# Ten tiles' transposes of p: from TensorE to 32x32 blocks on VectorE and a pass through DRAM

## The chip, the cores and the metric

The kernel runs on one core of a Trainium2 chip, as one program. The metric is the device time of an execution in microseconds (us). Times of a kernel are given as the median of a few executions, with the lowest and highest. One execution each is recorded by the hardware profiler; its trace is what is read below. The engines are named as in the profile: PE is TensorE's matmul, PEld its weight load, DVE VectorE, ACT ScalarE, POOL GpSimd, SP SyncE, which issues all DMAs of this kernel.

## The reference

Two layers of the same kind, each of a Fourier mixing and of a retrieval of experts by product keys, with residuals, on x of 2048 tokens by 512. `dft_*` are fixed matrices; there are 32 heads, 16 x 16 experts, and of each side's 16 keys the two best are kept, then the two best of their four sums (`top_s`, and their experts `top_e`).

```python
def _A_ref(x, dft_seq_re, dft_seq_im, dft_hid_re, dft_hid_im):
    a = jnp.einsum("bsd,ed->bse", x, dft_hid_re)
    b = jnp.einsum("bsd,ed->bse", x, dft_hid_im)
    return jnp.einsum("ts,bse->bte", dft_seq_re, a) - jnp.einsum("ts,bse->bte", dft_seq_im, b)

def _B_ref(x, w_q, k1, k2, u, v):
    ...
    q = jnp.einsum("nd,dhc->nhc", xf, w_q)
    s1 = jnp.einsum("nhd,ed->nhe", q[..., :dk], k1)
    s2 = jnp.einsum("nhd,ed->nhe", q[..., dk:], k2)
    ...
    g = _softmax(top_s, axis=-1)
    act = _gelu(jnp.einsum("nd,nhkd->nhk", xf, u[top_e]))
    return jnp.einsum("nhk,nhk,nhkd->nd", g, act, v[top_e])

for layer in range(2):
    x = x + _A_ref(_layernorm(x), ...)
    x = x + _B_ref(_layernorm(x), ...)
```

## The kernel before, in words

**Numbers.** Everything is float32 in accuracy: an operand is split into a high part and a low part (`xh` and `xl`, `ch` and `cl`, and so on), and a product is three matmuls: high by high, high by low, low by high.

**Tiles.** The tokens are 16 tiles of 128. The mixing over the sequence (`seq_unit`, matmuls at L515) makes a unit of two tiles at a time: it streams the sequence matrix (`raw`, 256 KB pieces, L451), splits it on ScalarE (`ch`, L455) and VectorE (`cl`, L459), and accumulates in the four `acc` banks. The units of layer 0 are made in order; unit n holds tiles 2n and 2n + 1, and the last two tiles are units of their own. Then `token_tile` does the rest for one tile:

- L656: the mixing over the hidden dimension; L666 adds it to `row`; then the layer norm, x in `xn` (L268).
- x transposed. From the third unit of layer 0 on (`MOVED`) this goes through DRAM: VectorE turns 32x32 blocks (L712), SP writes `xdr` (L716) and reads it back in four pieces with the blocks put in their places (L725), ScalarE and VectorE split it (`tok`, L732 and L735).
- L774 and L778: x by the folded query and key weights, in two halves; L783 copies the scores to `sc`. L805: x by u, copied to `act` (L810), and the gelu in a few steps on ScalarE and VectorE (L818 to L825).
- VectorE's search for the best scores (L864 to L953), transposes of the codes q on TensorE (L986), one-hot rows `lr` (L1009, L1015) and small matmuls (L1025) that make the gate matrix. It goes through DRAM into token layout: `gdr` (L1035, L1055) and `gt` (L1063).
- L1065: `act` times `gt` on VectorE. The result is p, 128 tokens by 256 experts.
- p transposed (L1093), split (L1098, L1101), and p by v (L1112, L1116; p@v below). L1127 adds it to `row`, L1137 stores the row.

In layer 1, the first seven of the nine units (13 tiles) are `DEFERRED`: p is turned by blocks on VectorE (L1072), split (L1076, L1079), written to DRAM, and taken up at the end of the program.

**What sets the order.** The program is written down as operations with an engine, an estimated duration, predecessors and buffers (`op`, `Hold`). `Plan.run` places them one after another on the engines by their estimated times; the instructions are then issued in the order of these estimated starts. On the chip every engine takes its instructions in exactly this order and waits where an operand is not there. A change of a few operations therefore moves many others. SP too takes its DMAs in order; a DMA that waits for a semaphore holds up those behind it.

**Buffers that matter here:** one of `gt` and one of `pp` (the split p), three of `act`, four PSUM banks called `bank`, four of `raw`.

In the code printed here `deferred` and `moved` are set at L610 and L611, the deferred end of p is L1070 to L1088, and the part for all other tiles is L1090 to L1105.

## Time and profile before

| | us |
|---|---|
| median of 3 executions | 1258.39 |
| lowest and highest | 1256.29, 1258.56 |
| the profiled execution: its own time | 1259.73 |
| the profiled execution: span from first to last instruction | 1257.7 |

How it is read: a row of the costliest groups has line, engine and operation, output<-inputs, shape and count, then busy time and mean duration of one, then the idle time of the engine just before these instructions and who ended it. A row of the timeline has the start, the duration, and engine, line, operation and tiles. Matmuls are pipelined: each shows longer than the distance to the next, so the price of one is read from starts, not from durations.

```profile
L656 PE MATMUL bank<-dh,pth 128*128 128x512 f32 (+1 forms) x264 | 102.5, 390 | 3.6 <-ACT pth L540 3.6
L774 PE MATMUL bank<-wh,tok 128*128 128x512 f32 x256 | 100.4, 392 | 1.0 <-ACT tok L732 1.0
...
L1009 DVE TENSOR_TENSOR lr<-iota,qt 128x1024 f16<-128x1024 f16 x124 | 80.0, 684 | 10.8 <-ACT qt L990 10.8
```

### The profile page before, as it was taken

How to read it: one execution, taken by the hardware profiler on the slowest of the kernel's cores; microseconds unless marked ns; L12 is line 12 of the kernel's file. 1: busy time of each engine (PE TensorE's matmuls, PEld its weight loads, DVE VectorE, ACT ScalarE, POOL GpSimd, SP SyncE). 2: the span in 40 equal slices, each digit the busy share in tenths (PEclk: the TensorE clock that was granted, in tenths of full speed). 3: DMA queues.
4: the chain of work that ended last, by engine and by line, in shares of the span. 5: the costliest groups of instructions: out<-in, count | busy, mean ns of one | idle time of the engine just before them, and what ended most of it. 6: DMA issues, size and time to landing. Idle time of an engine off the chain costs nothing.

```text
span 1257.7 us, 20768 instructions
## 1 busy us (share of the span) xinstructions
PE 1234.3 (98%) x7601; PEld 1019.9 (81%) x7601; DVE 1011.2 (80%) x2290; ACT 481.3 (38%) x994; POOL 46.4 (4%) x71
## 2 busy tenths in 40 slices
PE   9999999999999999999999999999999999999988
PEld 6877778777787888799878888888888888888875
DVE  8899997988897786859976479777786959587777
ACT  7522244343333333333564243333333434334433
POOL 2000000000000000000000000000000000000000
PEclk9999999999999999999999999999999999999999
DMA  7866551333334233342465333525344342515654
GB/s 235 259 198 222 182 156 32 87 93 90 96 90 94 83 94 91 93 110 68 120 157 143 101 84 100 134 61 131 87 112 115 84 126 87 145 55 107 142 121 126
DMA packets 317765, 148.18 MB, mean 118 GB/s; under 512 B 221920, under 2 KB 287968, under 8 KB 317664
## 3 DMA queue, kind: packets, MB, share of 16 engines
q1 hardware_dynamic: 317664, 146.87, 43.9%
q8 instruction: 59, 0.97, 0.3%
q14 instruction: 42, 0.34, 0.1%
HBM read 120.86 MB, written 25.95 MB: 117 GB/s over the span
## 4 chain that ended last, share of the span: by engine, by line
PE 77%; DVE 14%; DMA 3%; issue 2%; SPq 2%; ACT 1%; POOL 1%; DVEq 0%; ACTq 0%
PE acc L515 40%; PE bank L656 11%; PE bank L774 8%; PE bank L778 4%; PE bank L805 3%; DVE cl L459 2%; PE bank L515 2%; DVE w L381 1%; PE bank L1112 1%; PE bank L389 1%; PE bank L1025 1%; DMA raw<-x2d 1%; DVE eq L882 1%; DVE eq L858 1%; PE acc L588 1%
## 5 line engine op out<-in xcount | busy, mean ns | idle before, releaser
L515 PE MATMUL acc<-ch,xh 128*128 128x512 f32 (+1 forms) x868 | 328.5, 378 | 0.2 <-DVE ptl L543 0.2
L515 PE MATMUL acc<-ch,xl 128*128 128x512 f32 (+1 forms) x868 | 321.8, 371 | 0.0
L515 PE MATMUL acc<-cl,xh 128*128 128x512 f32 (+1 forms) x868 | 321.8, 371 | 0.0
L455 ACT CAST ch<-raw 128x512 fp32r<-128x512 f32 x256 | 158.4, 619 | 276.8 <-PE acc L515 217.1
L459 DVE TENSOR_TENSOR cl<-raw,ch 128x512 fp32r<-128x512 f32 x256 | 174.7, 685 | 47.9 <-ACT ch L455 46.7
L515 PEld LDWEIGHTS acc<-cl,xh 128*128 128x128 f32 x868 | 163.5, 188 | 28.6
L515 PEld LDWEIGHTS acc<-ch,xh 128*128 128x128 f32 x868 | 163.7, 189 | 27.2 <-DVE ptl L543 1.1
L515 PEld LDWEIGHTS acc<-ch,xl 128*128 128x128 f32 x868 | 163.9, 189 | 25.2
L656 PE MATMUL bank<-dh,pth 128*128 128x512 f32 (+1 forms) x264 | 102.5, 390 | 3.6 <-ACT pth L540 3.6
L774 PE MATMUL bank<-wh,tok 128*128 128x512 f32 x256 | 100.4, 392 | 1.0 <-ACT tok L732 1.0
L656 PE MATMUL bank<-dl,pth 128*128 128x512 f32 (+1 forms) x264 | 101.0, 384 | 0.0
L774 PE MATMUL bank<-wl,tok 128*128 128x512 f32 x256 | 99.8, 390 | 0.0
L864 DVE TENSOR_TENSOR tmp<-sc 128x512 f32<-128x512 f32 (+1 forms) x66 | 44.3, 672 | 65.7 <-ACT sc L783 64.8
L656 PE MATMUL bank<-dh,ptl 128*128 128x512 f32 (+1 forms) x264 | 95.6, 384 | 0.0
L1009 DVE TENSOR_TENSOR lr<-iota,qt 128x1024 f16<-128x1024 f16 x124 | 80.0, 684 | 10.8 <-ACT qt L990 10.8
L257 POOL TENSOR_TENSOR stats<-stats,half 128x1 f32<-128x1 f32 x64 | 45.1, 708 | 1163.6 <-DVE stats L254 1158.6
L783 ACT COPY sc<-bank 128x512 f32<-128x512 f32 x64 | 36.3, 588 | 134.0 <-PE bank L778 65.2
L858 DVE TENSOR_TENSOR eq<-sc,val 128x1024 f16<-128x1024 f32 (+1 forms) x66 | 78.6, 1192 | 1.8
L515 PE MATMUL acc<-ch,xg 128*128 128x512 f32 (+1 forms) x204 | 77.4, 380 | 0.0
L515 PE MATMUL acc<-cl,xg 128*128 128x512 f32 (+1 forms) x204 | 75.9, 372 | 0.0
L515 PE MATMUL acc<-ch,xm 128*128 128x512 f32 (+1 forms) x204 | 75.7, 371 | 0.0
L778 PE MATMUL bank<-wh,tok 128*128 128x512 f32 x256 | 68.4, 389 | 0.0
(166 smaller groups left out, 2057.4 us busy)
## 6 DMA issues: line engine op xcount, KB each, us to landing
raw<-in_cseq SPq DMA_DIRECT2D x224, 256.0 KB, 2.8
wr<-in_wq SPq DMA_DIRECT2D x32, 512.0 KB, 4.0
raw<-in_ctile SPq DMA_DIRECT2D x32, 256.0 KB, 2.9
xdr<-lr SPq DMA_DIRECT2D x25, 256.0 KB, 2.3
tok<-xdr SPq DMA_DIRECT2D x100, 64.0 KB, 2.6
wr<-in_x SPq DMA_DIRECT2D x16, 256.0 KB, 3.2
row<-in_x SPq DMA_DIRECT2D x16, 256.0 KB, 3.2
x2d<-row SPq DMA_DIRECT2D x16, 256.0 KB, 2.2
```

What stands on the lines that cost most here:

```text
L257: nc.gpsimd.tensor_tensor(st[:, 1:2], st[:, 1:2], half, op=ALU.pow)
L455: nc.scalar.copy(t[1], t[0])
L459: nc.vector.tensor_sub(t[2], t[0], as32(t[1]))
L515: nc.tensor.matmul(target(d), w[s][:, d * P:(d + 1) * P], moving(s % per, part), start=(s == 0 and k == 0 and d % blocks == 0), stop=(s == ...
L656: nc.tensor.matmul(t["y", cs.start], w[:, k, c, t0:t0 + P], r[:, c, k, cs], start=(z == 0 and c == 0 and m == 0), stop=(z == len(steps) - ...
L774: nc.tensor.matmul(t["pc", hf], t["th"][:, k, :], r[:, k, hf], start=(k == 0 and r is wh), stop=False)
L778: nc.tensor.matmul(t["pc", hf], t["tl"][:, k, :], wh[:, k, hf], start=False, stop=(k == KD - 1))
L783: nc.scalar.copy(t["sc"][:, :, hf, :], t["pc", hf].rearrange("p h e -> p e h"))
L805: nc.tensor.matmul(t["xu"], w[:, k, :], r[:, k, :], start=(m == 0), stop=(m == 3 * KD - 1))
L858: nc.vector.tensor_tensor(t["eq"][:, :, cols], flat("sc")[:, :, cols], val(rank_, cols), op=ALU.is_equal)
L864: nc.vector.tensor_max(t["tmp"][:, :, cols], flat("sc")[:, :8, cols], flat("sc")[:, 8:, cols])
L1009: nc.vector.tensor_tensor(t["m", hf, r], io2, row_of(r, hf), op=ALU.is_equal)
```

## The change

In layer 0, for units 2 to 6 (tiles 4 to 13, ten tiles), p is no longer transposed on TensorE. VectorE turns p in 32x32 blocks from `act` into `gt`; SP writes this to a DRAM tile `pdr` (128 KB, each partition 1 KB in a run) and reads it back into `act` in four pieces (32 KB, runs of 32 elements), which puts the blocks in their places. Then the high part is cast from `act` on ScalarE and the low part subtracted on VectorE, in place of the same two steps from PSUM. `gt` is held until the write has landed, `act` until the low part is made, and no PSUM bank is taken for it. The other tiles are as before. The planner is told of the new operations, so that it makes a new order; the orders are alike until 339 us of the profile before and from 682 us on.

```diff
+def P_MOVED(layer, at):
+    return layer == 0 and 2 <= at < 7
...
-            "tok": 3, "sc": 1, "eq": 1, "act": 3, "q": 2, "top": 1, "qt": 1, "lr": 4, "gt": 1, "pp": 1, "gdr": 2, "xdr": 2, "late": 3, "ev": 3, "bn": 1}
+            "tok": 3, "sc": 1, "eq": 1, "act": 3, "q": 2, "top": 1, "qt": 1, "lr": 4, "gt": 1, "pp": 1, "gdr": 2, "xdr": 2, "pdr": 2, "late": 3, "ev": 3, "bn": 1}
...
-        deferred = DEFERRED(layer, at)
+        deferred, p_moved = DEFERRED(layer, at), P_MOVED(layer, at)
...
-               back + [a_act], last=[] if deferred else [hgt], prio=prio)
+               back + [a_act], last=[] if deferred or p_moved else [hgt], prio=prio)
...
-        a = op("PE", 2 * TR32, f_pt, [a], take=[hb], last=[hact], prio=prio)
-        a_ph = op("ACT", act(N), f_ph, [a], take=[hpp], prio=prio)
-        a = op("DVE", dve(N), f_pl, [a_ph], last=[hb], prio=prio)
+        if p_moved:
+            hdp = Hold("pdr")
+
+            def f_turn():
+                nc.vector.transpose(t["gt"].rearrange("p e f -> p (e f)"), t["act"])
+
+            def f_out():
+                t["pdr"] = dram.tile([4, 32, 2, 4, 32], F32, name="pdr", bufs=BUFS["pdr"])
+                nc.sync.dma_start(t["pdr"].rearrange("i d k j t -> (i d) (k j t)"), t["gt"].rearrange("p e f -> p (e f)"))
+
+            a = op("DVE", dve(N), f_turn, [a], prio=prio)
+            b = op("SP", load(128), f_out, [a], take=[hdp], last=[hgt], prio=prio, lag=2.3)
+            back = []
+            for j in range(4):
+                def f_in(j=j):
+                    nc.sync.dma_start(t["act"][32 * j:32 * j + 32].rearrange("p (k i t) -> p k i t", i=4, t=32),
+                                      t["pdr"][:, :, :, j, :].rearrange("i d k t -> d k i t"))
+                back.append(op("SP", 0.3, f_in, [b], behind=back[-1:], last=[hdp], prio=prio, lag=2.8))
+
+            def f_ph():
+                t["pp"] = work([P, 2, N], F32R, "pp")
+                t["ph"], t["pl"] = (t["pp"][:, m].rearrange("p (k t) -> p k t", t=P) for m in range(2))
+                nc.scalar.copy(t["pp"][:, 0], t["act"])
+
+            def f_pl():
+                nc.vector.tensor_sub(t["pp"][:, 1], t["act"], as32(t["pp"][:, 0]))
+
+            a_ph = op("ACT", act(N) + 0.05, f_ph, back, take=[hpp], prio=prio)
+            a = op("DVE", dve(N), f_pl, [a_ph], last=[hact], prio=prio)
+        else:
+            a = op("PE", 2 * TR32, f_pt, [a], take=[hb], last=[hact], prio=prio)
+            a_ph = op("ACT", act(N), f_ph, [a], take=[hpp], prio=prio)
+            a = op("DVE", dve(N), f_pl, [a_ph], last=[hb], prio=prio)
```

What moves is seen at tile 4, the first of the ten, on SP's queue and on TensorE. SP before, in the program's order around this place (numbers of the code before): tile 6's x is read back, raw pieces are loaded, tile 5's gates are written, tile 7's x is written, tile 4's row is stored, tile 5's gates are read.

```order
L725 DMA tok<-xdr 32x16x32 x4
L451 DMA raw<-in_cseq 128x2x256 x3
L1055 DMA gdr<-sc 32x16x16 x4
L716 DMA xdr<-lr 128x512
L1137 DMA x2d<-row 128x512
L1063 DMA gt<-gdr 64x16x16 x2
```

In the change (its own line numbers; L1115 is p's write, L1122 its reads):

```order
L729 DMA tok<-xdr 32x16x32 x4
L455 DMA raw<-in_cseq 128x2x256 x2
L1115 DMA pdr<-gt 128x256
L455 DMA raw<-in_cseq 128x2x256
L1059 DMA gdr<-sc 32x16x16
L1122 DMA act<-pdr 32x8x32 x4
L1059 DMA gdr<-sc 32x16x16 x3
L720 DMA xdr<-lr 128x512
```

p's five DMAs have come in between the raw loads and the gate writes of tile 5, and the store of tile 4's row (L1171 in the change) has gone behind tile 5's gates and tile 7's x.

On TensorE, p@v of tile 4 stood between the two halves of tile 6's query matmuls:

```order
L774 MATMUL bank<-wl,tok 128x512
L778 MATMUL bank<-wh,tok 128x512 x4
L1112 MATMUL bank<-vh,pp 128x512
L1112 MATMUL bank<-vl,pp 128x512
L1112 MATMUL bank<-vh,pp 128x512
L1112 MATMUL bank<-vl,pp 128x512
L1116 MATMUL bank<-vh,pp 128x512 x2
L774 MATMUL bank<-wh,tok 128x512
```

In the change it stands behind both halves and behind tile 6's product with u (L809 now), ahead of the sequence matmuls (L519 now):

```order
L809 MATMUL bank<-ul,tok 128x256
L809 MATMUL bank<-uh,tok 128x256
L1146 MATMUL bank<-vh,pp 128x512
L1146 MATMUL bank<-vl,pp 128x512
L1146 MATMUL bank<-vh,pp 128x512
L1146 MATMUL bank<-vl,pp 128x512
L1150 MATMUL bank<-vh,pp 128x512 x2
L519 MATMUL acc<-ch,xh 128x512
```

Twelve of the query matmuls and the twelve of the product with u now go ahead of it.

## The prediction

> **What bounds the kernel now.** The page comes first: its span, the engines' busy time, the granted clock, the chain that ended last and the costliest group.
>
> ```profile
> span 1257.7 us, 20768 instructions
> ...
> PE 1234.3 (98%) x7601; PEld 1019.9 (81%) x7601; DVE 1011.2 (80%) x2290; ACT 481.3 (38%) x994; POOL 46.4 (4%) x71
> ...
> PEclk9999999999999999999999999999999999999999
> ...
> PE 77%; DVE 14%; DMA 3%; issue 2%; SPq 2%; ACT 1%; POOL 1%; DVEq 0%; ACTq 0%
> ...
> L515 PE MATMUL acc<-ch,xh 128*128 128x512 f32 (+1 forms) x868 | 328.5, 378 | 0.2 <-DVE ptl L543 0.2
> ```
>
> TensorE is busy 98% of the span at full clock, carries 77% of the chain, and its largest group waits 0.2 us in all. So TensorE's instruction stream is the bound: what leaves it is time, what makes it wait is time, and work on the other engines counts only where TensorE waits for it.
>
> Next, where. The instruction orders of the two programs agree up to the transposes of tile 4 (the fifth), at 339 us, and again from 682 us. The view of busy time by windows gives that stretch.
>
> ```profile
> core 0: us, PE busy (x) PEld busy (x) DVE busy (x) ACT busy (x) POOL busy (x), PEclk, DMA share, GB/s
> 339.00:682.00 343.00, 338.17 (x2079) 285.02 (x2080) 272.95 (x649) 139.76 (x289) 12.16 (x20) 1.00 0.41 104
> ```
>
> TensorE is idle 343.00 - 338.17 = 4.83 us there. This and the removed work is all that can be won; VectorE has 70 us free.
>
> **What leaves TensorE.** Two float32 transposes for each of ten tiles. Their cost is read from the starts around one pair, in the timeline of TensorE; an ordinary step in those rows is 0.23 us (392.31 to 392.54).
>
> ```profile
> 392.31 0.39 PE L515 MATMUL acc<-ch,xl 128*128 128x512 f32 x1
> 392.54 0.39 PE L515 MATMUL acc<-cl,xh 128*128 128x512 f32 x1
> 392.77 0.38 PE L1093 MATMUL bank<-identf,act 128*128 128x128 f32 x2
> 392.90 0.48 PE L515 MATMUL acc<-ch,xh 128*128 128x512 f32 x1
> 393.22 0.39 PE L515 MATMUL acc<-ch,xl 128*128 128x512 f32 x1
> ```
>
> From 392.54 to 393.22 are 0.68 us; two ordinary steps are 0.46, so the pair costs 0.22 us, although the two show as 0.38 (they overlap their neighbours). Ten tiles: **-2.2 us**.
>
> The groups of TensorE between 338 and 641 us, shapes apart, give its waits in front of these transposes, of x's query matmuls (the transfer path that x already takes), and of q's transposes.
>
> ```profile
> L774 PE MATMUL bank<-wh,tok 128*128 128x512 f32 x72 | 28.3, 393 | 1.0 <-ACT tok L732 1.0
> ...
> L1093 PE MATMUL bank<-identf,act 128*128 128x128 f32 x20 | 4.0, 283 | 2.2 <-DVE act L1065 2.0
> ...
> L986 PE MATMUL bank<-ident,q 128*128 128x128 f16 x27 | 3.1, 223 | 0.7 <-DVE q L953 0.3
> ```
>
> The transposes waited 2.2 us, nearly all for VectorE's multiply by the gates (L1065). With them gone TensorE no longer stops there: **-2.2 us**. What is late next is p itself, in front of p@v.
>
> **What is added, and where it lies.** Per tile: one 32x32-block transpose on VectorE, one 128 KB write, four 32 KB reads; the high and low parts are then made from SBUF in place of PSUM. The deferred tiles of layer 1 already run the same compute instructions.
>
> ```profile
> L1072 DVE STREAM_TRANSPOSE gt<-act x13: 400/439/446, 777.3 to 1158.1; 128x256 f32<-128x256 f32 x13
> ```
> ```profile
> L1076 ACT CAST pp<-gt x13: 392/406/409, 778.2 to 1159.1; 128x256 fp32r<-128x256 f32 x13
> ```
> ```profile
> L1098 ACT CAST pp<-bank x19: 353/372/377, 240.2 to 1251.8; 128x256 fp32r<-128x256 f32 x19
> ```
> ```profile
> L1079 DVE TENSOR_TENSOR pp<-gt,pp x13: 392/419/425, 779.0 to 1159.8; 128x256 fp32r<-128x256 f32 x13
> ```
>
> VectorE gets 10 x 0.44 = 4.4 us, ScalarE 10 x 0.03. I cost both at nothing: VectorE is busy 273 of 343 us, and its wait rows that reach TensorE are small (0.7 us in front of q's transposes). If that cover were gone, all 4.4 us would come out in front of q; nothing, the end nearest to the 0.7 row, is taken. The PSUM bank that the transposes no longer take is worth nothing beyond this: waits for it stood in front of the transposes and are within the 2.2.
>
> The transfers have no rows of their own; x's path has, with twice the bytes and the same 128-byte pieces. These are its reads and its writes in the window, with their times from issue to landing.
>
> ```profile
> L725 SPq DMA_DIRECT2D tok<-xdr x36: 568/634/1502, 348.2 to 636.9; - x36
> ...
> DMA to landing us min/median/max: 2.3/2.7/3.7
> ```
> ```profile
> L716 SPq DMA_DIRECT2D xdr<-lr x9: 339/563/677, 345.3 to 631.9; - x9
> ...
> DMA to landing us min/median/max: 2.0/2.2/2.9
> ```
>
> Undisturbed, then, p is ready about 0.44 + 2.2 + 3 x 0.63 (three issues ahead of the last read) + 2.7 + 0.41 + 0.42 = 8.1 us after the multiply, and half a microsecond more for the hand-overs. The tighter the order puts p@v behind that, the more TensorE waits.
>
> A rule of the Trainium skill speaks against this path. "VectorE: DVE Perf Modes", section "The three transpose paths", says that a plain copy that transposes by access-pattern strides is 19 times slower than the hardware's DMA transpose where the innermost destination stride is large; 19 times the 1309 ns that it lists would be an estimated 25 us a tile. The rows disagree with that for these pieces: the strided reads of x land in 2.7 us, since runs of 32 elements stay together and VectorE turns within the blocks. By the rule the sum would gain well over 100 us; by the rows it stays as follows.
>
> **Tile 4 in full.** The section on the change shows its rows: p@v moves behind the second half of tile 6's query matmuls and its x@u; on SP, p's write goes behind two raw loads, its reads behind the third raw load and one gate write. The timelines of SP, VectorE and TensorE give the times.
>
> ```profile
> 338.28 4.14 SPq L451 DMA_DIRECT2D raw<-in_cseq  x3
> 342.52 2.66 SPq L1055 DMA_DIRECT2D gdr<-sc  x4
> ```
> ```profile
> 338.49 0.42 DVE L1065 TENSOR_TENSOR act<-act,gt 128x256 f32<-128x256 f32 x1
> ...
> 341.34 0.68 DVE L459 TENSOR_TENSOR cl<-raw,ch 128x512 fp32r<-128x512 f32 x1
> ```
> ```profile
> 343.61 0.40 PE L1112 MATMUL bank<-vh,pp 128*128 128x512 f32 x1
> ...
> 345.01 0.39 PE L774 MATMUL bank<-wh,tok 128*128 128x512 f32 x1
> ...
> 349.17 0.40 PE L515 MATMUL acc<-ch,xh 128*128 128x512 f32 x1
> ```
>
> The multiply ends at 338.91, the turn at 339.4. SP's third raw load waits for its buffer (freed by L459 at 342.02), so the gate write is issued at 342.52 as now and the reads from 343.2 (2.66 / 4 later); p's write has landed by then. The last read goes out at 345.1 and lands at 347.8; cast, subtraction and hand-overs make 349.0. TensorE reaches p@v when x@u ends: 349.17 now, less the 1.40 us of p@v (343.61 to 345.01) that no longer stands ahead: 347.8. **Wait: 1.2 us.** The three gate writes behind the reads, and so tile 5's gates and its multiply, go 2.7 us later; tile 5's p@v has itself moved behind tile 7's query matmuls and covers that.
>
> On ScalarE the cast of p, which now waits for the reads, stands ahead of tile 6's score copies:
>
> ```profile
> 346.79 0.59 ACT L783 COPY sc<-bank 128x512 f32<-128x512 f32 x1 [3.51 <-DMA gdr<-sc]
> 347.93 0.59 ACT L783 COPY sc<-bank 128x512 f32<-128x512 f32 x1 [0.56 <-PE bank L778]
> ```
>
> With the cast from 347.9 to 348.3 the second copy ends near 349.5 instead of 348.5, and VectorE's search for tile 6's largest scores starts 1.0 us late. That reaches TensorE only as a wait in front of q's transposes, the 0.7 row; I count nothing, and 1.0 as the other end. Behind p@v on TensorE stand sequence matmuls, which lose the 1.2 us and no more.
>
> For the other nine tiles the bounds are nothing (the order puts p@v later than p can be ready) and tile 4's 1.2 us. The nearest row is x's: 72 of these matmuls are nine tiles (8 each), 1.0 us of wait in all, 0.11 a tile. I take that: 9 x 0.11 = 1.0. New waits: 1.2 + 1.0 = **+2.2 us**, between 0 and 12.
>
> **Sum.** -2.2 - 2.2 + 2.2 = -2.2 us. The profiled execution took 1259.73 us (1257.7 of span and 2.0 around it) and would take 1257.5. It lies 1.3 above the median of 1258.39; the same difference from the median gives **1256.2 us**. A measurement of this kernel can tell about 0.2% (2.5 us) from no change, so this counts as no change.
>
> **Rivals.**
> - *The waits go too.* All ten tiles wait like x's, 1.1 us: -2.2 - 2.2 + 1.1 = -3.3, 1255.1 us, and up to -7.0 if every idle microsecond of the window went with them. For it: x's wait row, and nine tiles whose p@v was also moved back. Against it: the 1.2 us counted for tile 4.
> - *The work that leaves TensorE returns as idle time,* because the tile chain through VectorE and SP sets the pace there: 1258.4 us. For it: TensorE's waits were all for VectorE. Against it: VectorE's 70 idle us.
> - *SP's queue makes p late everywhere (slower).* Nine of the ten pairs of write and reads have other transfers between them in the new order, most often a raw load, which waits for its buffer. If all nine wait as tile 4 does: 9 x 1.2 + 0.1 = 10.9, less 4.4: +6.5, 1264.9 us. It is level at 0.44 us a tile and slower by 0.2% from 0.69. For it: reads of x took up to 1.5 us to issue. Against it: x's 0.11 a tile on the same queue. On this side stands also a line of the same page of the Trainium skill, section "Rules for kernel authors": a 128x128 transpose belongs on TensorE where a PSUM destination is acceptable. No price for a TensorE that is the bound goes with it.
> - *The transposes stay:* excluded by the order, in which 20 fewer stand.
>
> **Chances.** Forecast 0.43, the waits go too 0.32, returned as idle time 0.13, slower 0.12. The forecast's low side (0.08) lies beyond 0.2%: faster 0.32 + 0.08 = 0.40; no change 0.35 + 0.12 = 0.47; slower 0.12 + 0.01 = 0.13. The range reaches from the deeper half of the first rival, -6, to about half of the slower one's way, +2.3: 1252.4 to 1260.7. The forecast's own is 1254.5 to 1257.8.
>
> **What would show it.** TensorE's transposes of `act` fall from 38 to 18. In the window PE's busy time falls by 2.2 us. Idle time in front of L1146 should be near 2.2 us, most of it at tile 4 near 348 us; if it is above 5, SP's queue is the cause and its rows show late reads; if it is under 1, the first rival holds. Wrong in kind I would be if TensorE came to wait for raw loads (L519), or for q (L990) by more than 2 us, which I cost at nothing.

## The result, and the profile after

| | median us | lowest to highest | runs |
|---|---|---|---|
| before, run beside it | 1257.84 | 1256.29 to 1258.56 | 4 |
| the change, undisturbed | 1265.54 | 1263.60 to 1266.42 | 3 |
| the change, run again later | 1268.77 | 1267.46 to 1269.38 | 4 |

The changed kernel is slower: 1.0063 of the kernel before, with a 95% interval of 1.0046 to 1.0080, and 1.0061 (1.0042 to 1.0079) when run again. That is some 8 us more, where 2 us less were forecast, and it lies above the range. The first recorded execution of the changed kernel was disturbed (3264.75 us), so the profile below is one of the same kernel recorded anew, whose own time is 1269.38 us. In the change's numbering the lines up to L1065 stand four further on: the sequence matmuls are L519, x's query matmuls L778 and L782, q's transposes L990, the small matmuls L1029. The turn is L1111, p's write L1115, its reads L1122, the cast L1129, the subtraction L1132, p@v L1146 and L1150.

The page of the changed kernel, span, engines and chain:

```profile
span 1267.3 us, 20841 instructions
...
PE 1236.4 (98%) x7581; PEld 1020.3 (81%) x7581; DVE 1014.5 (80%) x2300; ACT 483.0 (38%) x994; POOL 49.4 (4%) x71
...
PE 68%; DVE 18%; DMA 5%; SPq 4%; issue 3%; ACT 2%; POOL 1%; DVEq 0%; ACTq 0%
```

TensorE has 20 matmuls fewer (7581 against 7601) and yet shows 2.1 us more busy time. On the chain it has gone from 77% to 68%; VectorE, DMA and SP have taken its place. The stretch of the change, from the place where the two orders part to the place where they join again, ran from 338.97 to 681.91 us before and runs from 338.97 to 688.90 now: 342.94 us have become 349.93, **7.0 us more**. The view of busy time by windows for the changed kernel, the stretch first and a short piece of it second:

```profile
338.97:688.90 349.93, 339.19 (x2060) 284.65 (x2059) 274.60 (x655) 140.05 (x287) 14.65 (x19) 1.00 0.44 109
623.20:626.60 3.40, 3.40 (x14) 2.94 (x13) 1.37 (x3) 2.75 (x6) 0.00 (x0) 0.51 0.85 186
```

TensorE's idle time in the stretch is 349.93 - 339.19 = 10.74 us, where it was 4.8: **5.9 us more idle**. Its waits there, by who ended them (us, times, longest):

```profile
PE bank L1146 <- ACT pp L1129: 3.2, 2, 2.3
PE bank L778 <- ACT tok L736: 2.4, 4, 1.3
PE bank L990 <- DVE q L979: 2.0, 2, 1.2
PE bank L990 <- DVE q L957: 1.2, 2, 0.6
PE bank L1029 <- DVE lr L1019: 0.7, 1, 0.7
PE bank L782 <- DVE tok L739: 0.7, 1, 0.7
```

The waits in front of p's transposes are gone, as forecast (two transposes are left in the stretch, with no wait). In their place stand p@v with 3.2 us, in two places only, x with 2.4 + 0.7 = 3.1 us, and the search and its one-hot rows (q and `lr`) with 2.0 + 1.2 + 0.7 = 3.9 us; a last row has 0.3 us for `ptl` (L660). So **most of the new waiting isn't for p** but for two things that the change doesn't touch.

The first of p@v's two waits is the one worked out ahead, at tile 4. TensorE's timeline:

```profile
347.98 0.28 PE L809 MATMUL bank<-uh,tok 128*128 128x256 f32 x1
349.17 0.50 PE L1146 MATMUL bank<-vh,pp 128*128 128x512 f32 x1 [0.91 <-ACT pp L1129]
```

The second is at tile 12, and it shows a second price, a lower clock behind the wait. TensorE, then SP ahead of it:

```profile
622.70 0.51 PE L1146 MATMUL bank<-vh,pp 128*128 128x512 f32 x1 [2.31 <-ACT pp L1129]
...
625.87 0.41 PE L519 MATMUL acc<-ch,xm 128*128 128x256 f32 x1
626.08 0.41 PE L519 MATMUL acc<-cl,xg 128*128 128x256 f32 x1
```
```profile
614.25 0.33 SPq L1115 DMA_DIRECT2D pdr<-gt  x1
614.82 0.33 SPq L1186 DMA_DIRECT2D raw<-x2d  x1
616.21 0.38 SPq L455 DMA_DIRECT2D raw<-in_cseq  x1
616.99 0.60 SPq L1059 DMA_DIRECT2D gdr<-sc  x1
617.64 2.59 SPq L1122 DMA_DIRECT2D act<-pdr  x4
```

p's reads go out at 617.64, 3.1 us behind the write, with a raw load that waited for its buffer between them. After 2.3 us without work the granted clock of TensorE is about half for 3.4 us (0.51 in the windows above): steps of 0.12 us become 0.21 (625.87 to 626.08), which costs 3.4 x (0.21 - 0.12) / 0.21 = 1.5 us. That is one part of why TensorE's busy time in the stretch rose by 1.1 us (338.1 to 339.2) although 2.2 us of work had left it; the other part is worked out further below.

### The profile page after: what moved, and what is told of

Read it like the earlier page. It is cut to its first block, busy times and chain, and to the rows that moved or that the text cites. A ratio compares the mean times of both kernels' runs of the same rounds, so it can differ in the third digit from the quotient of the medians.

```text
span 3262.6 us, 20841 instructions
## 1 busy us (share of the span) xinstructions
PE 3257.0 (100%) x7581; PEld 2058.1 (63%) x7581; DVE 1042.2 (32%) x2300; ACT 486.8 (15%) x994; POOL 43.8 (1%) x71
## 4 chain that ended last, share of the span: by engine, by line
PE 100%; DVE 0%; POOL 0%; issue 0%; POOLq 0%
PE acc L519 56%; PE bank L660 15%; PE bank L778 9%; PE bank L782 5%; PE bank L809 4%; PE bank L519 2%; PE bank L393 2%; PE acc L592 1%; PE bank L1146 1%; PE bank L1029 1%; PE acc L1232 1%; PE acc L499 1%; PE bank L1150 1%; PE bank L990 0%; PE acc L504 0%; PE bank L748 0%
## 5 line engine op out<-in xcount | busy, mean ns | idle before, releaser
L519 PE MATMUL acc<-ch,xh 128*128 128x512 f32 (+1 forms) x868 | 704.0, 811 | 0.0
L519 PE MATMUL acc<-cl,xh 128*128 128x512 f32 (+1 forms) x868 | 700.0, 806 | 0.0
L519 PE MATMUL acc<-ch,xl 128*128 128x512 f32 (+1 forms) x868 | 699.3, 806 | 0.0
L519 PEld LDWEIGHTS acc<-cl,xh 128*128 128x128 f32 x868 | 326.1, 376 | 184.5 <-issue 179.4
L519 PEld LDWEIGHTS acc<-ch,xl 128*128 128x128 f32 x868 | 328.4, 378 | 169.3 <-issue 169.3
L519 PEld LDWEIGHTS acc<-ch,xh 128*128 128x128 f32 x868 | 324.7, 374 | 170.6 <-issue 168.4
L660 PE MATMUL bank<-dh,pth 128*128 128x512 f32 (+1 forms) x264 | 222.3, 843 | 0.0
L660 PE MATMUL bank<-dl,pth 128*128 128x512 f32 (+1 forms) x264 | 222.3, 842 | 0.0
L660 PE MATMUL bank<-dh,ptl 128*128 128x512 f32 (+1 forms) x264 | 214.2, 841 | 0.0
L778 PE MATMUL bank<-wh,tok 128*128 128x512 f32 x256 | 212.3, 829 | 0.0
L778 PE MATMUL bank<-wl,tok 128*128 128x512 f32 x256 | 212.1, 829 | 0.0
L782 PE MATMUL bank<-wh,tok 128*128 128x512 f32 x256 | 167.2, 828 | 0.0
L519 PE MATMUL acc<-ch,xg 128*128 128x512 f32 (+1 forms) x204 | 165.2, 810 | 0.0
L519 PE MATMUL acc<-ch,xm 128*128 128x512 f32 (+1 forms) x204 | 164.3, 806 | 0.0
L519 PE MATMUL acc<-cl,xg 128*128 128x512 f32 (+1 forms) x204 | 164.0, 804 | 0.0
L660 PEld LDWEIGHTS bank<-dl,pth 128*128 128x128 f32 x264 | 96.7, 366 | 59.3 <-issue 59.3
L660 PEld LDWEIGHTS bank<-dh,ptl 128*128 128x128 f32 x264 | 93.7, 362 | 64.0 <-issue 58.8
L660 PEld LDWEIGHTS bank<-dh,pth 128*128 128x128 f32 x264 | 96.0, 364 | 59.8 <-issue 57.8
L782 PEld LDWEIGHTS bank<-wh,tok 128*128 128x128 f32 x256 | 90.9, 355 | 61.7 <-issue 58.7
L778 PEld LDWEIGHTS bank<-wh,tok 128*128 128x128 f32 x256 | 90.3, 353 | 60.2 <-issue 58.8
```

Source lines behind the costliest of these rows:

```text
L519: nc.tensor.matmul(target(d), w[s][:, d * P:(d + 1) * P], moving(s % per, part), start=(s == 0 and k == 0 and d % blocks == 0), stop=(s == ...
L660: nc.tensor.matmul(t["y", cs.start], w[:, k, c, t0:t0 + P], r[:, c, k, cs], start=(z == 0 and c == 0 and m == 0), stop=(z == len(steps) - ...
L778: nc.tensor.matmul(t["pc", hf], t["th"][:, k, :], r[:, k, hf], start=(k == 0 and r is wh), stop=False)
L782: nc.tensor.matmul(t["pc", hf], t["tl"][:, k, :], wh[:, k, hf], start=False, stop=(k == KD - 1))
```

## What the rivals are, and the runs

Four theories, each with its place:

- **A, p is late.** The trip through DRAM is longer than the place that the order gives it, and ScalarE's cast and TensorE's p@v stand and wait for it.
- **B, the order.** The planner's new order is worse in itself, whatever p does.
- **C, SP's queue.** p's five DMAs hold up others on SP's in-order queue: those of x and of the gates come late.
- **D, VectorE's turn.** The 4.4 us of added VectorE work come out on TensorE.

All ratios are to the kernel before on the same chip, three rounds each, with the 95% interval. A ratio of 0.001 is 1.3 us. Where the planner is told something else it makes another order; the runs `o_none`, `o_load`, `o_issue` and `o_pool` share one order of every other instruction, as `wide` and the changed kernel share theirs.

| run | what differs | ratio | interval |
|---|---|---|---|
| `again` | the changed kernel | 1.0061 | 1.0042 to 1.0079 |
| `lag` | p later in the plan | 1.0032 | 1.0021 to 1.0043 |
| `order` | new order, transposes on TensorE, no turn, no DMA of p | 0.9988 | 0.9977 to 0.9998 |
| `o_turn` | `order` with the turn | 0.9989 | 0.9978 to 0.9999 |
| `o_none` | `o_turn`, transposes somewhat earlier | 0.9997 | 0.9988 to 1.0007 |
| `o_load` | `o_none` with p's DMAs, not waited for | 1.0094 | 1.0076 to 1.0112 |
| `o_issue` | `o_load`, DMAs without their own waits | 1.0094 | 1.0072 to 1.0116 |
| `o_pool` | `o_load`, DMAs on GpSimd's queue | 1.0034 | 1.0023 to 1.0045 |
| `wide` | the change, half the pieces in p's reads | 1.0031 | 1.0020 to 1.0042 |
| `wide_lag` | `wide` and `lag` | 1.0014 | 1.0005 to 1.0024 |
| `told` | the planner told SP's real time | 1.0079 | 1.0062 to 1.0096 |
| `upto6` | eight tiles in place of ten | 1.0038 | 1.0024 to 1.0053 |
| `extra` | kernel before, with p's trip besides | 1.0086 | 1.0071 to 1.0101 |
| `poolq` | the change with p's DMAs on GpSimd's queue | 1.0159 | 1.0135 to 1.0182 |

### The change again, and p planned later

`again` is the changed kernel without an edit.

> The changed kernel once more, unedited, for a profile at full matmul rate (in the profiled execution above a matmul took 0.81 us on average where before's took 0.38, so its waits can't be compared). Theory A (p is late: SP's queue holds its write and reads behind raw loads and gate writes, and TensorE waits in front of p@v): the idle time of PE in front of L1146 in the ten tiles is 8 to 11 us in all. Theory B (the new order is at fault elsewhere: q, x or the gates come late because the queues were rearranged): L1146 waits under 3 us, and the idle time stands in front of L990, L778, L1029 or L519. Both: PE busy in the window of the change 2.2 us less than before, time 1263 to 1267 us, ratio 1.005 to 1.008.

Measured: 1.0061; its profile is the one above.

`lag` makes the planner wait 2 us longer for p's reads:

```diff
-                back.append(op("SP", 0.3, f_in, [b], behind=back[-1:], last=[hdp], prio=prio, lag=2.8))
+                back.append(op("SP", 0.3, f_in, [b], behind=back[-1:], last=[hdp], prio=prio, lag=4.8))
```

> The changed kernel, with the planner's estimate for the landing of p's reads raised from 2.8 to 4.8 us; nothing else. In the trace of the rerun the way from the turn to the cast of p takes 6.8 to 9.2 us, while the planner's own figures add up to about 7.1. Theory A (p comes later than planned; ScalarE and SP, which take their work in order, stand before it, and x, q and p@v behind them are late): the planned 9.1 covers the trip, ScalarE's 22.8 us of idle time in front of p's cast fall below 5, TensorE's idle time in the window returns to about before's, and the time comes out at 0.998 to 1.001 of before. Theory B (the order that the planner made is at fault apart from p): another order, so no firm number, 1.002 to 1.008. Theory C (the five DMAs and the turn load SP and VectorE): unchanged, 1.005 to 1.008.

Measured: 1.0032, half of the loss gone. It does act on p's way: who waited for p's reads, and for how long, in the changed kernel first and in `lag` second:

```profile
  ACT pp L1129: 22.8, 9
```
```profile
  ACT pp L1129: 3.7, 4
```

ScalarE stood idle in front of p's cast for 22.8 us, at nine of ten tiles, and now for 3.7. But TensorE's wait for p isn't smaller in `lag`: 4.5 us in two places, against 3.2. What fell are the waits for q and `lr`, from 3.9 us to 0.5. Work on ScalarE and VectorE that was queued behind the waiting cast would fit that, but it isn't shown: at tile 6 ScalarE copies the scores at 350.7 us in the changed kernel and at 349.9 in `lag`, both times after a wait for tile 5's gate writes on SP's queue, and in `lag`, whose order is another, TensorE comes to that tile's q only when it is there (370.5, no wait). How large A's share is stays open.

### Is it the order, or the turn?

`order` keeps the changed kernel's plan and its order but transposes p on TensorE, at the place of the last read, and leaves turn and DMAs out; `o_turn` puts the turn back.

```diff
             def f_turn():
-                nc.vector.transpose(t["gt"].rearrange("p e f -> p (e f)"), t["act"])
+                pass
             def f_out():
+                return
...
                 def f_in(j=j):
+                    if j == 3:
+                        f_pt()
+                    return
...
-                nc.scalar.copy(t["pp"][:, 0], t["act"])
+                nc.scalar.copy(t["ph"], t["pt"])
```

> The changed kernel's plan, and so its order on every engine, but the data path of before: the turn, the write and the reads are left out, and TensorE transposes p into PSUM at the place in the order where the last read stood, about 3 us ahead of the cast. Theory A: p is ready when its cast comes up, the waits for x, q and p go; 2.2 us of transposes come back: 1.000 to 1.002 of before. Theory B: the order alone costs what the change costs, and 2.2 us more: 1.006 to 1.009. Theory C: as A.

> As the run `order` (the changed kernel's order on all engines, p transposed on TensorE, no turn and no transfers: 0.9988 of before), but with the ten turns on VectorE done as well, into gt, which nothing reads. Theory D (the cost is VectorE's: 4.4 us of turns in front of q and x): 1.002 to 1.005. Theories A (late p) and C (transfers in SP's queue): VectorE has room, 0.998 to 1.000.

Measured: 0.9988 and 0.9989, both a little faster than the kernel before (their intervals end at 0.9998 and 0.9999), though TensorE does all its transposes. TensorE's waits in the stretch of `order`:

```profile
PE bank L660 <- ACT pth L544: 2.1, 1, 2.1
PE bank L990 <- DVE q L957: 0.5, 1, 0.5
PE bank L778 <- ACT tok L736: 0.4, 1, 0.4
```

**B and D fall.** The new order is at least as good as the old one: no wait in front of the transposes is left there either, so that gain needed no transfer, only a later place. And the 4.4 us on VectorE cost nothing that these two runs can tell apart (0.9988 and 0.9989, each known to about 0.001).

### The DMAs alone

`o_load` makes the turn, the write and the reads in their places, while p itself is transposed on TensorE ahead of the first read; nobody waits for what the DMAs bring, though buffers are held for them. `o_none` is the same kernel with the DMAs left out.

```diff
+                    if j == 0:
+                        f_pt()
                     nc.sync.dma_start(t["act"][32 * j:32 * j + 32].rearrange("p (k i t) -> p k i t", i=4, t=32),
                                       t["pdr"][:, :, :, j, :].rearrange("i d k t -> d k i t"))
...
-                nc.scalar.copy(t["pp"][:, 0], t["act"])
+                nc.scalar.copy(t["ph"], t["pt"])
```

> As `order`, with the turn, the write and the four reads done in their places too; TensorE transposes p just ahead of the first read, the split is from PSUM, and nothing but the buffers waits for the transfers. Theory A (late p: ScalarE, TensorE and VectorE stand before it): 0.998 to 1.001, as nobody stands before p any more. Theory C (the transfers in SP's in-order queue make x and the gates late, whoever reads p): 1.004 to 1.008, with the waits in front of the query matmuls and q's transposes still there. Between the two, the share of each is read off: the change has about 1.006 here, `order` 0.999.

> The kernel of o_load with p's five DMAs a tile left out and nothing else changed: the order of all other instructions is the same. If the DMAs on SP's queue are the loss of o_load (1.0094): 0.998 to 1.001. If o_load's place for TensorE's transposes carries the part that o_pool kept (1.0034): 1.002 to 1.004.

Measured: 1.0094 with the DMAs, 0.9997 without. Fifty DMAs that nobody waits for cost 0.97%, **12 us**, more than the whole loss of the change. TensorE's waits in the stretch, `o_load` first:

```profile
PE bank L778 <- ACT tok L736: 4.9, 5, 2.0
PE bank L1029 <- DVE lr L1019: 2.1, 1, 2.1
```
```profile
PE bank L778 <- ACT sc L1039: 1.8, 1, 1.8
PE bank L778 <- ACT tok L736: 0.8, 1, 0.8
```

x's wait (`tok`) goes from 0.8 us to 4.9. The changed kernel shows how, at tile 9's x, which VectorE has turned by 404.9 us. SP's timeline of the changed kernel, then of `o_none` at the same place, where all is 3.4 us earlier (the turn ends at 401.5):

```profile
405.36 2.59 SPq L1122 DMA_DIRECT2D act<-pdr  x4
408.05 0.55 SPq L455 DMA_DIRECT2D raw<-in_cseq  x1
408.70 2.64 SPq L1059 DMA_DIRECT2D gdr<-sc  x4
411.44 0.56 SPq L720 DMA_DIRECT2D xdr<-lr  x1
...
417.69 0.34 SPq L1115 DMA_DIRECT2D pdr<-gt  x1
418.08 2.64 SPq L729 DMA_DIRECT2D tok<-xdr  x4
```
```profile
401.54 2.83 SPq L1059 DMA_DIRECT2D gdr<-sc  x4
404.47 0.56 SPq L720 DMA_DIRECT2D xdr<-lr  x1
...
409.42 2.66 SPq L729 DMA_DIRECT2D tok<-xdr  x4
```

Without p's DMAs x's write is issued 3.0 us after the turn and its reads start 7.9 us after it. With them p's reads and the gate writes that they push back stand ahead: the write goes out 6.5 us after the turn, the reads start after 13.2 us, behind p's next write, which waited for its own turn. TensorE stands at the end of that line:

```profile
423.45 0.50 PE L778 MATMUL bank<-wh,tok 128*128 128x512 f32 x1 [1.29 <-ACT tok L736]
```

From the starts and landings of all ten of these trips in the trace (VectorE's turn of x ends, last of x's four reads landed; tiles 6 to 15), the mean trip is 11.5 us in `o_none`, 12.6 in the changed kernel and 13.1 in `o_load`. The transfers themselves were not slower: x's reads took 2.7 us at the median from issue to landing in all three.

x isn't all of it. The stretch takes 354.3 us in `o_load` and 341.3 in `o_none`: 13.0 us more, of which 8.3 are idle time of TensorE, and 4.9 of these are waits for `tok` (L778 and L782); the other 4.7 us are longer busy time of TensorE. The same queue also holds up q. There is one buffer `sc`, and tile 6's scores can be copied into it only when tile 5's gate writes, which read it, have landed. Three of these four writes stand behind p's four reads. ScalarE's copies of tile 6's scores, `o_load` first:

```profile
351.06 1.08 ACT L787 COPY sc<-bank 128x512 f32<-128x512 f32 x2 [7.02 <-DMA gdr<-sc]
```
```profile
347.14 1.07 ACT L787 COPY sc<-bank 128x512 f32<-128x512 f32 x2 [3.31 <-DMA gdr<-sc]
```

They come 3.9 us later with p's DMAs than without. In the changed kernel they start at 350.7 (346.8 before), and TensorE then waits 0.64 and 0.78 us for tile 6's q at 370 us: 1.4 of the 3.9 us for q and `lr`.

### Issue time, or waiting in the queue?

SP may lose its time by issuing or by standing in front of a DMA whose data isn't there. `o_issue` is `o_load` with other data in p's DMAs (a constant written, pieces of the input read, nobody uses either), so that they don't wait for the turn or for the write:

```diff
-                nc.sync.dma_start(t["pdr"].rearrange("i d k j t -> (i d) (k j t)"), t["gt"].rearrange("p e f -> p (e f)"))
+                nc.sync.dma_start(t["pdr"].rearrange("i d k j t -> (i d) (k j t)"), as32(uh[:, 0]))
...
-                                      t["pdr"][:, :, :, j, :].rearrange("i d k t -> d k i t"))
+                                      x_in[64 * i:64 * i + 64].rearrange("q (h f) -> (q h) f", h=2).rearrange("(i d) (k j t) -> i d k j t", i=4, k=2, j=4)[:, :, :, j, :].rearrange("i d k t -> d k i t"))
```

> The kernel of o_load with p's write fed from a constant in place of the turned p, and p's four reads fed from the input x in place of the written p. Same number, sizes and places of the DMAs on SP's queue, same order on every engine; but the write no longer waits for VectorE's turn, and the reads no longer wait for the write to land (they still wait for TensorE's transposes, which read the buffer that they overwrite). Nothing uses what they carry. Theory C has two forms. C-wait: the DMAs behind p's stand behind a DMA that waits (for the turn, for the landing): then this is 0.999 to 1.003 of the kernel before, and x's wait on TensorE falls from 5.8 us to under 1.5. C-issue: the five DMAs take some 2.8 us of SP's time a tile, and that alone is too much: then it stays at 1.006 to 1.010, and x's wait stays above 4.

`o_pool` is `o_load` with these five DMAs issued by GpSimd, at the same places:

```diff
-                nc.sync.dma_start(t["pdr"].rearrange("i d k j t -> (i d) (k j t)"), t["gt"].rearrange("p e f -> p (e f)"))
+                nc.gpsimd.dma_start(t["pdr"].rearrange("i d k j t -> (i d) (k j t)"), t["gt"].rearrange("p e f -> p (e f)"))
...
-                    nc.sync.dma_start(t["act"][32 * j:32 * j + 32].rearrange("p (k i t) -> p k i t", i=4, t=32),
+                    nc.gpsimd.dma_start(t["act"][32 * j:32 * j + 32].rearrange("p (k i t) -> p k i t", i=4, t=32),
```

> The kernel of o_load with p's five DMAs issued from GpSimd's queue at the same places of the program, so that SP's queue is that of o_turn while every transfer of p is still made and waited for by buffers alone. Theory C (SP's in-order queue, by either form): 0.998 to 1.003, x's wait on TensorE under 1.5 us. Rival: the transfers themselves (DMA engines, memory, the later release of buffers) do the harm: 1.006 to 1.010 as o_load. A third way, GpSimd's small additions for the layer norm now stand behind waiting DMAs on its queue: then the loss shows as waits in front of the sequence matmuls or of x's transfer, with L261 ahead of them.

Measured: `o_issue` 1.0094, no better than `o_load`, and x's wait is 6.5 us there (4.9 in `o_load`); `o_pool` 1.0034, just above the range expected for C. Moving the same transfers off SP's queue, with the buffers held as before, takes away 0.6 of the 0.94%, and x's trip is back at 11.4 us with a wait of 1.4 us. What is left in `o_pool`, 0.37% over `o_none`, is in small waits (1.3 us more on the mixing, 0.5 on p's low part, 0.5 more on `lr`, 0.6 more on x) whose cause I did not separate. In `o_issue` SP still waits in front of p's DMAs, but less than half as long; the longest rows of SP's own waits there, `o_load` and then `o_issue` (in these two kernels p's reads are L1124):

```profile
SPq L1124 <- PE bank L1097: 6.2, 4, 2.2
...
SPq L1115 <- DMA gt<-gdr: 4.9, 3, 2.3
SPq L1115 <- DVE gt L1111: 4.8, 4, 1.4
...
SPq L1124 <- DMA pdr<-gt: 3.7, 3, 2.1
```
```profile
SPq L1124 <- PE bank L1097: 9.8, 4, 3.9
...
SPq L1124 <- DVE gt L1111: 1.0, 1, 1.0
```

23.1 us of such waits (these four rows of `o_load` and three smaller ones, 3.5 us in all) became 10.8 and nothing was won. What remains is nearly all for TensorE's transposes, 9.8 us; that wait belongs to these two kernels, and the change has none. It grew from 6.2, so this run separates issue time and waiting only in part. It speaks for **the time that SP needs to issue them** as the larger cause, and `wide` below tests that in the changed kernel. These are the rows of p's write and reads in the changed kernel (minimum, median and maximum in ns):

```profile
L1115 SPq DMA_DIRECT2D pdr<-gt x10: 319/344/441, 339.6 to 630.6; - x10
```
```profile
L1122 SPq DMA_DIRECT2D act<-pdr x40: 557/612/684, 344.5 to 635.3; - x40
```

0.34 + 4 x 0.61 = **2.8 us of SP's queue a tile**; the planner counts 0.3 for a read.

### The change with fewer pieces

If SP's time is what counts, it can be made shorter in the changed kernel itself. `wide` permutes the columns of `act` (j k d in place of k j d), so that a read moves runs of 64 elements: 128 pieces in place of 256, the same bytes and the same order. Two of the places where the code changes:

```diff
-                nc.scalar.copy(t["act"], t["xu"])
+                nc.scalar.copy(t["act"].rearrange("p (j k d) -> p k j d", k=2, d=32),
+                               t["xu"].rearrange("p (k j d) -> p k j d", j=4, d=32))
...
-                    nc.sync.dma_start(t["act"][32 * j:32 * j + 32].rearrange("p (k i t) -> p k i t", i=4, t=32),
-                                      t["pdr"][:, :, :, j, :].rearrange("i d k t -> d k i t"))
+                    nc.sync.dma_start(t["act"][32 * j:32 * j + 32].rearrange("p (i n) -> p i n", n=64),
+                                      t["pdr"][:, :, j].rearrange("i d n -> d i n"))
```

> The changed kernel, same order on every engine, with the columns of act permuted so that the two halves of a 32-expert block lie side by side: p's reads then move runs of 64 elements (256 bytes) in place of 32, 128 pieces a read in place of 256, with the same bytes, the same number of DMAs and the same waits. If SP needs its time by the piece, a read is issued in 0.30 to 0.40 us in place of 0.61, some 1 us a tile is saved on SP's queue, and the loss falls to between a third and two thirds: 1.002 to 1.004. If SP's time goes by the DMA, or the loss is in the waits between p's steps: 0.55 to 0.65 us a read and 1.005 to 1.007.

> The kernel of wide with the planner's lag of p's reads 2 us longer (4.8 in place of 2.8), as in the run lag. Lag alone brought the changed kernel from 1.0061 to 1.0032, the wider runs alone to 1.0031. If the two halves are separate (p too early in the order; SP's time for p's pieces), they add: 0.999 to 1.0015 of the kernel before. If both only spread the same lateness: 1.002 to 1.004.

Measured: `wide` 1.0031, half of the loss gone. Its reads on SP:

```profile
L1133 SPq DMA_DIRECT2D act<-pdr x40: 319/430/1718, 344.1 to 630.4; - x40
```

0.43 us in place of 0.61 (a little more than the 0.30 to 0.40 expected), 0.7 us a tile. x's mean trip falls from 12.6 to 12.0 us, and TensorE's wait for it from 2.4 to 0.4 us. Per microsecond of SP's queue a tile the two comparisons agree: `o_load` against `o_none` 12 us for 10 x 2.8, `wide` against `again` 3.8 us for 10 x 0.7, about half of it each time. Not all of the 3.8 need be issue time, though: `wide`'s reads also land 0.4 us sooner (2.0 us after their issue in place of 2.4), and TensorE's wait for p falls from 3.2 us to 1.5. With the later plan as well, `wide_lag` comes to 1.0014, beyond what each does alone though not the sum of both (1.0002). That fits two partial cures of mostly different lateness, and there is still no gain over the kernel before.

### Four runs that say less

`told` gives the planner 0.62 us for a read, `upto6` moves eight tiles instead of ten, `extra` adds turn, write and reads to the kernel before, whose own path for p stays, and `poolq` is the changed kernel with p's DMAs planned on GpSimd's queue.

```diff
+                back.append(op("SP", 0.62, f_in, [b], behind=back[-1:], last=[hdp], prio=prio, lag=2.5))
...
+    return layer == 0 and 2 <= at < 6
...
+                back.append(op("POOL", 0.3, f_in, [b], behind=back[-1:], last=[hdp], prio=prio, lag=2.8))
```

> The changed kernel with the planner told what SP needs for one of p's reads: 0.62 us in place of 0.3 (lag 2.5 in place of 2.8, so that a read is due at the same time after its issue begins). If the planner's figure is at fault, the new order leaves SP the room: 0.998 to 1.002 of the kernel before. If SP's queue has no room for 2.8 us a tile in this stretch however the order is made, or the trip is too long for it: 1.003 to 1.008, with x, gates or p again in TensorE's waits.

> The change for units 2 to 5 only (tiles 4 to 11); tiles 12 and 13 keep TensorE's transposes. In the rerun the longest single wait, 2.5 us for p at 620 us, and 1.0 us at half clock just behind it belong to tile 12. Theory A: about 3.5 to 4 of the 8 us go: 1.002 to 1.004. Theories B and C, with the cost spread over the ten tiles: a fifth goes: 1.004 to 1.007.

> The ten tiles keep TensorE's transposes and the split from PSUM, as before; the turn into gt, the 128 KB write and the four reads (back into act, which nothing reads any more) are done besides, and nobody waits for them but the buffers gt and act. Theory A: the load itself is harmless: 0.999 to 1.002. Theory C: it costs what the change costs and the 2.2 us that were not saved: 1.005 to 1.010. Theory B says nothing on it, as the order is a third one.

> The changed kernel with p's five DMAs a tile issued from GpSimd's queue, and planned there; SP's queue holds only what it held before. Theory C: SP free of them, x and the gates come as before; what is left is p's own lateness: 1.000 to 1.003. Theory A: p is no earlier, so 1.004 to 1.008; later still if GpSimd issues more slowly than SP's 0.6 us a read.

Measured: `told` 1.0079, so the right figure doesn't cure it; with it the planner made an order with as much waiting (x 3.6 us, `lr` 3.0). `upto6` 1.0038: a fifth fewer tiles, and a loss of 0.38% in place of 0.61%; with its interval this lies in the range expected for A as well as in that for B and C, so it decides nothing. `extra` 1.0086: the work alone, with nobody waiting for p, makes the kernel before slower by at least as much as the change is, as `o_load` then showed without another order (here TensorE waits 6.9 us for the multiply by the gates, whose transfers are on SP's queue). `poolq` 1.0159 was a miss: with p really needed, GpSimd's queue makes p late, and TensorE waits for it:

```profile
PE bank L1146 <- ACT pp L1129: 12.3, 6, 3.8
```

Its timeline at tile 5 shows the small additions of the layer norm between p's DMAs, and gaps between reads:

```profile
355.31 0.58 POOL L1115 DMA_DIRECT2D pdr<-gt  x1 [8.99 <-DVE gt L1111]
356.71 0.67 POOL L261 TENSOR_TENSOR stats<-stats,half 128x1 f32<-128x1 f32 x1 [0.82 <-DVE stats L258]
358.76 1.85 POOL L1122 DMA_DIRECT2D act<-pdr  x3 [1.38 <-DMA pdr<-gt]
362.02 0.59 POOL L1122 DMA_DIRECT2D act<-pdr  x1 [1.42 <-issue]
```

Of all versions only `order` and `o_turn` beat both kernels, by about 0.1% over the kernel before: p's transposes stay on TensorE and merely stand later. That is under the 0.2% that one such comparison tells apart with certainty.

## Why the prediction was wrong

- **20 transposes leave TensorE, -2.2: held.** The trace has 20 fewer. No kernel measured their price by itself; from the start of each to the next matmul, the 21 of them that the trace of before shows in the stretch take 2.0 us, 0.19 a pair, near the 0.22 taken.
- **The waits in front of them go, -2.2: held**; over the whole stretch they had been 3.1 us. `order` shows that they go without the change too, by a later place.
- **Tile 4 waits 1.2 us at 347.8: held.** 0.91 us of idle time ahead of 349.17, 1.07 from start to start. In part this is luck: p's reads went out at 344.5 instead of 343.2 and the last landed at 348.6 instead of 347.8, since SP stood longer in front of a gate write; against that, the first matmul of p@v waited only for the cast, not for the subtraction (0.42 us), which the sum had put in front of it.
- **Nine other tiles at 0.11 a tile, 1.0: mis-sized.** Eight of them wait for nothing, tile 12 for 2.3 us. p's own waits are 3.2 us where 2.2 were counted. The size was near, by luck: the mechanism, many small waits, was not what happened.
- **The failed step: what I costed at nothing.** "The three gate writes behind the reads, and so tile 5's gates and its multiply, go 2.7 us later" was seen at one tile and taken as covered, without asking what else waits for these writes: the scores of tile 6, which the forecast had 1.0 us late at the far end, were copied 3.9 us later, as the one `sc` was not free; and x, which has the same queue, was used as the measure of how little a transfer costs ("72 of these matmuls are nine tiles (8 each), 1.0 us of wait in all") without asking what becomes of x when 2.8 us a tile of other issues stand ahead of it. x went from 1.0 to 3.1 us of wait, q and `lr` from 0.7 to 3.9: +5.3 us at zero in the sum. Over the whole stretch the idle time adds up as -3.1 for the transposes, +3.2 for p, +5.3 for these and +0.3 for `ptl` (an operand of the hidden mixing): +5.7, of 5.9 measured; the forecast had it at zero. To it come 1.5 us of half clock, which I had not thought of, and 1.8 us for matmuls that start again after a wait: 0.16 us between the idle time and the time from start to start (0.91 and 1.07 above) and 0.10 at the next step (349.17 to 349.50 is 0.33 us in place of 0.23), at 13 waits in place of 6. -2.2 + 5.9 + 1.5 + 1.8 = 7.0. Another 2.6 us of that one execution, the slowest of its four, lie behind the stretch. Most of them are one wait of 1.8 us for x in layer 1 (825.7 us), where no other run's profile shows more than 0.74, and a second 3.4 us at half clock near the end, where before has one; why they came isn't known.
- **VectorE's 4.4 us at nothing: held** by `o_turn`. **ScalarE at nothing: failed in part.** ScalarE stood 22.8 us in front of the cast, and tile 6's scores were late; what those scores waited for last was the gate writes, not the cast, and how much of TensorE's loss goes back to the cast is not shown.
- **The rival on SP's queue** named the queue and the sign and gave 1264.9, near the 1265.5 measured, but by another mechanism: it made p late at every tile. p was late at two. The queue was right, who waits behind it wasn't, and that the number came so near is luck.
- **The 19-fold rule** of the Trainium skill ("VectorE: DVE Perf Modes", section "The three transpose paths") gave an estimated 25 us a tile. p's reads landed in 2.4 us at the median, so the estimate was far off for this path. That is no measurement against the rule: it names a large innermost stride at the destination, and here runs of 32 elements lie together there. The line of the same page, section "Rules for kernel authors", that a 128x128 transpose belongs on TensorE where its result may go to PSUM agrees with the times measured here (1.0061 for the change, 0.9988 for `order`).
- **What would show it:** transposes 38 to 18, seen; the fall of PE's busy time by 2.2 us was wrong (it rose by 1.1, with the half clock and the restarts); idle in front of L1146 was between the two bounds that I set, so by itself it would have told little; and the sentence "Wrong in kind I would be if TensorE came to wait ... for q (L990) by more than 2 us" came true with 3.2 us.

## What to carry to other kernels

Before work is moved from the bound engine to DMAs, add up what their issue costs on the queue that carries them (here 2.8 us a tile, 2.4 of it for reads in small pieces) and look for what stands behind them there; a transfer that nobody waits for can still cost the bound engine time, here nearly half of its issue time (12 us of 28). Ask also which buffers the DMAs behind it still read (here `sc`). A path that waits little today is no measure of a second path through the same queue: here it was x, with 1.0 us of wait before, that became late when the second was added. A wait in front of an operation may go by placing the operation later; try that before moving it to another engine.

## What the runs showed of the hardware that I had not expected

- A wait of TensorE can be followed by slow work: after 2.31 us idle (620.4 to 622.7) the granted clock was about half for 3.4 us, after 3.9 us (1203.8) for 6.8. In the profiles of all these kernels, past the first 100 us and ahead of the program's end, such a stretch followed only idle gaps of 1.8 us or more, and of the gaps over 2.7 us all but one were followed by it. A wait of that length can cost 1.5 us more than it shows. The Trainium skill, "TensorE: Matmul & The Clock Gate", section "HAM oscillation — how this bites in real kernels", asks for no idle gap above about 3.4 us; here 2.3 us was enough.
- SP's time for a DMA doesn't follow its bytes: 0.61 us for 32 KB in 256 pieces of 128 bytes, 0.43 us for 32 KB in 128 pieces of 256 bytes, 0.34 us for 128 KB in 128 pieces of 1 KB. Nor does it follow the number of pieces alone, as the expectation of `wide` had it: a raw load of 256 KB in 256 pieces of 1 KB takes 0.38 us. From issue to landing p's three differ little (2.4, 2.0 and 1.7 us).
- GpSimd's queue issues a read in nearly the same time (0.62 us in `poolq`) but a write in 0.60 in place of 0.34, and leaves gaps of about a microsecond, up to 2.1, in front of reads for which the profile shows no cause (`issue`, 12.9 us in 11 places in `poolq`).
